# Retention and routed experts on one core: state products as four quarters, and the last chunk's routing logits for all batches together

## The chip, the cores and the metric

The kernel runs on one core of one Trainium2 chip. The metric is the time of the whole program on the device in microseconds (us). Engines: TensorE (PE: products, and PEld: loading of the stationary operand), VectorE (DVE), ScalarE (ACT), GpSimd (POOL) and the SP queue, which issues most DMAs.

## The reference

A retention layer is followed by a mixture of experts. For each of 4 batches and 8 heads a 64 x 64 state decays and takes up one outer product for each of 768 tokens; the output of a token is its query times the state:

```python
for t in range(S):                       # S = 768, D = 64
    state = gamma * state + einsum('bhd,bhe->bhde', k[:, :, t], v[:, :, t])
    y[:, :, t] = scale * einsum('bhd,bhde->bhe', q[:, :, t], state)
```

The 8 heads' outputs of a token, side by side, are a row of 512 numbers. These 3072 rows go to 8 experts:

```python
logits = x @ w_gate                      # 3072 x 8
# all (token, expert) pairs in falling order of logit: a token goes to the first
# expert that still has room (384 rows each)
out[mask] = maximum(x[mask] @ w1[e], 0) @ w2[e]     # 512 -> 1024 -> 512
```

## The kernel before

**Units.** The sequence is cut into 6 chunks `c` of 128 tokens. A unit `u = 4 c + b` is chunk `c` of batch `b`, 24 in all. Heads go in pairs `pr` (4 of them); of a pair, head `s = 0` lies on partitions 0 to 63 and head `s = 1` on 64 to 127. Units 0 to 7 are worked one by one, those after it in pairs (8, 9), (10, 11), ... (22, 23): these are the 16 `groups`. Even places of a pair are even batches, odd ones odd batches.

**One unit** (all in fp32; TensorE works a product in two records in the trace):
- `load` (L256) brings 1 MB of keys, queries and values (768 KB for the last chunk) into one of 8 buffers `ld`, by the SP queue. The load of unit `u + 8` is issued when group work on unit `u` is done.
- `scores` (L288): keys times queries within the chunk, 8 products on 64 rows, `s` choosing the row half; VectorE multiplies the result by the decay mask (`am`, two instructions). GpSimd makes scaled keys `ks` and queries `qs`.
- `outputs` (L316): the part of the outputs that comes from the state. `T[b]` holds for each pair of heads a 128 x 128 block with the two 64 x 64 states on its diagonal and zeros elsewhere, so that one full 128 x 128 product serves both heads. It opens the sums in PSUM tile `yp` (two buffers, one bank each).
- `mix` (L329): scores times values, 8 products with 64 columns, `s` choosing the column half, on top of the same sums. `yp` is copied to `YS[b, c]` (feature by token; of the last chunk half by ScalarE, half by VectorE). The new part of the state, `sp`, is 8 more products, and VectorE adds it to the diagonal of `T[b]` (two instructions a unit, L357).

**Routing.** `gate(c)` (L395) multiplies the outputs of a finished chunk of all four batches by the gate weights `wgf`, 16 products that each fill 32 columns; ScalarE copies the result to `gs`, and `logit` transposes it later, so that logits stand by token. The last chunk goes another way: `gate_last(b)` (L361) takes a batch's `YS` as the stationary operand and 8 gate columns as the moving one, which gives logits by token at once, in units 20 and 21 during the last group and 22 and 23 at the end. Then VectorE takes the maximum of each token, compares it with a grid of 64 thresholds (`reach`) and 24 products count the tokens of each expert above each threshold (L494). A search follows that narrows the threshold twice more (`search`), and its result gives the first expert's rows.

**Rows to memory.** All outputs must lie in memory (`xs`) by token before the experts gather them. 14 units are turned by VectorE's 32 x 32 transposes (`row_blocks`, L384; `ROWS` says how many behind which group) and written by four DMAs of 64 KB each. The other 10 are turned by TensorE beside the search (`rows_out`: four transposes, a ScalarE copy, one DMA of 256 KB); `BESIDE` gives how many units and how many filler products stand before each step of the search. The buffers `xr` are six.

**What sets the order.** TensorE, VectorE and ScalarE follow the order of the code. In a group: scores of the next group, outputs of this one, one step of routing, mix, state, then loads and row transposes. The SP queue issues in the order of the code too; its DMAs take eight semaphores in turn, and each waits until the DMA eight places ahead of it has landed. The experts' stage follows a planner that the change doesn't touch.

Of the kernel before, what the change touches and what calls it, by code (L numbers as in the profile page):

```python
# [43 lines left out]
BESIDE = ((4, 0), (1, 0), (4, 0), (1, 0), (0, 6), (0, 10))  # L44
LEFT = sum(k for k, _ in BESIDE)
# [6 lines left out]
def tile_retention_moe(ctx: ExitStack, tc: tile.TileContext, qkv, wg, idm, w1, w2,  # L52
# [15 lines left out]
    wgf = consts.tile([128, HP, 32], F32, name="wgf")  # L68
# [180 lines left out]
    T = [rc.tile([128, HP, 128], F32, name=f"T{b}") for b in range(B)]  # L249
# [65 lines left out]

    def outputs(us):  # L316

        c = units[us[0]][1]
        for u in us:
            yp = yps[u] = rp.tile([128, HP, C], F32, name="yp", bufs=2)  # L320
            if c:
                b, qs = units[u][0], st[u][1]
                for pr in range(HP):
                    nc.tensor.matmul(yp[:, pr, :], T[b][:, pr, :], qs[:, pr, :], start=(pr == 0), stop=False,  # L324
                                     skip_group_check=True)
            else:
                busy(WARM[u + 1], yp[:, 0:2, :].rearrange("p a b -> p (a b)"))

    def mix(us):  # L329

        c = units[us[0]][1]
        for u in us:
            b, am, yp = units[u][0], st[u][0], yps.pop(u)
            v_ = LD[u][:, 2].rearrange("p (h d) -> p h d", h=H)
            for pr in range(HP):
                for s in range(2):
                    nc.tensor.matmul(yp[64 * s:64 * s + 64, pr, :], v_[:, 2 * pr + s, :], am[:, s, pr, :],  # L337
                                     start=(not c and pr == 0), stop=(pr == HP - 1), skip_group_check=True)
# [6 lines left out]
        if c < NC - 1:  # L345
# [7 lines left out]
            for i, u in enumerate(us):  # L353
                b = units[u][0]
                for s in range(2):
                    r = slice(64 * s, 64 * s + 64)
                    nc.vector.tensor_tensor(T[b][r, :, r], T[b][r, :, r], sp[r, i], op=OP.add)  # L357

    lt5 = []

    def gate_last(b):  # L361
        if not b:
            lt5.append(rp.tile([128, 64, E], F32, name="sp"))
        for pr in range(HP):
            nc.tensor.matmul(lt5[0][:, b, :], YS[b, NC - 1][:, pr, :], wgf[:, pr, 0:E], start=(pr == 0),  # L365
                             stop=(pr == HP - 1))
# [10 lines left out]
    def row_out(pr_, i):  # L377
        b, c = units[i]
        xr = xo.tile([128, DM], F32, name="xr")
        nc.scalar.activation(blocks(xr), pr_.rearrange("p (b a r) -> p b a r", a=4, b=HP), AF.Copy)  # L380
# [3 lines left out]
    def row_blocks(i):  # L384
# [6 lines left out]
        for a in range(4):  # L391
            nc.sync.dma_start(xs[t0:t0 + 128, 128 * a:128 * a + 128].rearrange("(t c) f -> c t f", t=4),
                              xr[32 * a:32 * a + 32].rearrange("p (t f) -> p t f", t=4))

    def gate(c):  # L395

        gl = rp.tile([128, 512], F32, name="gl")
        for pr in range(HP):
            for b in range(B):
                nc.tensor.matmul(gl[32 * b:32 * b + 32, 0:C], wgf[:, pr, :], YS[b, c][:, pr, :], start=(pr == 0),  # L400
# [23 lines left out]
    rowed = 0  # L424
    nu = len(units)
# [23 lines left out]
    with tc.manual_schedule(engines={nc.vector.engine, nc.scalar.engine}):  # L449
# [3 lines left out]
        for g, us in enumerate(groups):  # L453
# [9 lines left out]
            if g > B:  # L463
                if g == len(groups) - 1:
                    for u in groups[g - 1]:
                        gate_last(units[u][0])
# [8 lines left out]
            for _ in range(ROWS.get(g, 0)):  # L475
                row_blocks(rowed)
# [6 lines left out]
        for u in groups[-1]:  # L483
            gate_last(units[u][0])
        c = NC - 1
        cols, Lc = slice(c, COLS, NC), lt5[0][:, 0:B]
        f = best(Lc, cols, m0, oh0)
        reach(cols, B, m0, cmp0, grid[0])
        f()
        c0 = rp.tile([1 << QB[0], E], F32, name="gl")  # L490
        sg0 = sw.tile([1 << QB[0], E], BF, name="sg")
        order = [c for k in range(NC) for c in range(k, COLS, NC)]
        for k, c in enumerate(order):
            nc.tensor.matmul(c0, cmp0[:, c, :], oh0[:, c, :], start=(k == 0), stop=(k == COLS - 1))  # L494
# [409 lines left out]
    def rows_out(i):  # L904
        pr_ = pp.tile([128, DM], F32, name="py" if i % 2 else "ph", bufs=2 if i % 2 else 3)
# [33 lines left out]
    for rows, k in BESIDE:  # L939
        for _ in range(rows):  # L940
            rows_out(rowed)
# [222 lines left out]
```

## Time and profile before

| | us |
|---|---|
| median of 3 runs | 451.43 (449.72 to 455.44) |
| profiled execution | 449.59 |
| its span | 447.7 |
| TensorE busy | 431.4 (96%) |
| VectorE busy | 298.1 (67%) |
| ScalarE, GpSimd busy | 142.9 each (32%) |
| DMA share of q1, the SP queue's / of q0, GpSimd's | 20.5% / 29.9% of 16 engines' span |

The first stage (retention) ends at about 101 us of the span, the search for the first expert runs to 117 us, and the experts fill the rest. In the rows below a time is counted from the start of the span; "L337" is a line of the kernel; an arrow `out<-in` names the tile written and those read. In a timeline row, what stands in brackets at the end is the engine's idle time ahead of the row and what ended it. Matmul rows count records, two for each fp32 product.

### The profile page before, as it was taken

How to read it: one execution, taken by the hardware profiler on the slowest of the kernel's cores; microseconds unless marked ns; L12 is line 12 of the kernel's file. 1: busy time of each engine (PE TensorE's matmuls, PEld its weight loads, DVE VectorE, ACT ScalarE, POOL GpSimd, SP SyncE). 2: the span in 40 equal slices, each digit the busy share in tenths (PEclk: the TensorE clock that was granted, in tenths of full speed). 3: DMA queues.
4: the chain of work that ended last, by engine and by line, in shares of the span. 5: the costliest groups of instructions: out<-in, count | busy, mean ns of one | idle time of the engine just before them, and what ended most of it. 6: DMA issues, size and time to landing. Idle time of an engine off the chain costs nothing.

```text
span 447.7 us, 9118 instructions
## 1 busy us (share of the span) xinstructions
PE 431.4 (96%) x3745; PEld 374.7 (84%) x3747; DVE 298.1 (67%) x714; ACT 142.9 (32%) x221; POOL 142.9 (32%) x154
## 2 busy tenths in 40 slices
PE   8999999899999979999899999999999999999994
PEld 6899999898589758987788799789879989989983
DVE  1668688966989773875876789478678836416500
ACT  1111212115155132423431443343244436326301
POOL 2477655200520360026116016122501615502001
PEclk9999999998999995999999999999999999999998
DMA  7999987745680382038327436513813372831001
GB/s 252 409 416 413 367 272 222 217 90 196 213 281 13 135 280 91 1 119 285 115 94 228 171 119 172 206 49 121 297 77 117 84 294 70 287 160 47 1 25 53
DMA packets 23332, 78.99 MB, mean 176 GB/s; under 512 B 3058, under 2 KB 10866, under 8 KB 16884
## 3 DMA queue, kind: packets, MB, share of 16 engines
q0 software_dynamic: 8592, 46.14, 29.9%
q1 hardware_dynamic: 14692, 32.20, 20.5%
q8 instruction: 31, 0.51, 0.5%
q14 instruction: 17, 0.14, 0.1%
HBM read 65.75 MB, written 12.58 MB: 175 GB/s over the span
## 4 chain that ended last, share of the span: by engine, by line
PE 61%; issue 13%; DMA 12%; DVE 7%; POOL 3%; SPq 1%; ACT 1%; POOLq 0%; DVEq 0%
PE py L888 22%; PE ph L867 22%; DMA ld<-qkv 8%; PE psm L126 5%; PE yp L337 2%; PE pt L835 2%; DMA qtb<-qtab 2%; PE sc L295 2%; DVE w2l L126 2%; PE yp L324 1%; POOL out L896 1%; POOL wraw L783 1%; PE sp L351 1%; DMA xg<-xs,idx 1%; PE sp L365 1%
## 5 line engine op out<-in xcount | busy, mean ns | idle before, releaser
L867 PE MATMUL ph<-xh,w1h 128*128 128x384 f32 x256 | 86.2, 352 | 2.6 <-ACT xh L840 1.8
L867 PE MATMUL ph<-xlo,w1h 128*128 128x384 f32 x256 | 83.9, 341 | 0.0
L867 PE MATMUL ph<-xh,w1l 128*128 128x384 f32 x256 | 83.5, 341 | 0.0
L888 PE MATMUL py<-w2h,hh 128*128 128x512 f32 x192 | 78.4, 408 | 0.0
L888 PE MATMUL py<-w2l,hh 128*128 128x512 f32 x192 | 75.3, 392 | 0.6 <-DVE w2l L126 0.6
L888 PE MATMUL py<-w2h,hl 128*128 128x512 f32 x192 | 75.2, 392 | 0.0
L896 POOL DMA_INDIRECT out<-yo,oix x24 | 27.1, 1131 | 117.7 <-ACT yo L894 116.9
L871 ACT ACTIVATE hh<-ph 128x384 fp32r<-128x384 f32 x64 | 31.4, 491 | 84.4 <-PE ph L867 79.5
L783 POOL DMA_INDIRECT wraw<-w,wix x31 | 36.5, 1179 | 60.4 <-DVE un L126 52.6
L867 PEld LDWEIGHTS ph<-xh,w1h 128*128 128x128 f32 x256 | 48.3, 191 | 4.6 <-ACT xh L840 2.7
L867 PEld LDWEIGHTS ph<-xlo,w1h 128*128 128x128 f32 x256 | 48.6, 192 | 0.0
L867 PEld LDWEIGHTS ph<-xh,w1l 128*128 128x128 f32 x256 | 48.6, 191 | 0.0
L126 DVE SCALAR_TENSOR_TENSOR hl<-ph,hh 128x384 fp32r<-128x384 f32 x64 | 34.8, 552 | 17.1 <-ACT hh L871 16.8
L126 DVE TENSOR_TENSOR w1l<-wraw,w1h 128x1024 fp32r<-128x1024 f32 (+1 forms) x36 | 39.4, 1102 | 7.4 <-ACT w1h L801 7.4
L888 PEld LDWEIGHTS py<-w2l,hh 128*128 128x128 f32 x192 | 36.1, 188 | 7.9 <-DVE w2l L126 1.8
L888 PEld LDWEIGHTS py<-w2h,hl 128*128 128x128 f32 x192 | 36.0, 188 | 7.8
L822 POOL DMA_INDIRECT xg<-xs,idx x24 | 26.5, 1106 | 48.1 <-PE ph L867 34.3
L888 PEld LDWEIGHTS py<-w2h,hh 128*128 128x128 f32 x192 | 36.1, 188 | 6.4
L894 ACT ACTIVATE yo<-py 128x512 f32<-128x512 f32 x24 | 14.3, 598 | 83.9 <-PE py L888 40.2
L126 DVE TENSOR_TENSOR w2l<-wraw,w2h 128x1024 fp32r<-128x1024 f32 x32 | 38.8, 1217 | 1.3 <-ACT w2h L801 1.2
L801 ACT ACTIVATE w1h<-wraw 128x1024 fp32r<-128x1024 f32 (+1 forms) x36 | 33.7, 958 | 11.0 <-DMA wraw<-w,wix 9.4
L801 ACT ACTIVATE w2h<-wraw 128x1024 fp32r<-128x1024 f32 x32 | 33.4, 1053 | 0.0
(149 smaller groups left out, 607.0 us busy)
## 6 DMA issues: line engine op xcount, KB each, us to landing
ld<-qkv SPq DMA_DIRECT2D x19, 1024.0 KB, 10.8
xs<-xr SPq DMA_DIRECT2D x56, 64.0 KB, 3.9
ld<-qkv SPq DMA_DIRECT2D x4, 768.0 KB, 6.2
xs<-xr SPq DMA_DIRECT2D x10, 256.0 KB, 2.9
qtb<-qtab SPq DMA_DIRECT2D x5, 256.0 KB, 12.0
ld<-qkv SPq DMA_DIRECT2D x2, 512.0 KB, 5.5
wraw<-w,wix POOLq DMA_INDIRECT x33, 7.3
xg<-xs,idx POOLq DMA_INDIRECT x24, 3.7
```

Source lines behind the costliest of these rows:

```text
L126: return f(o, *a, **k)
L295: nc.tensor.matmul(sc[s][:, pr, :], k_[r, w], q_[r, w], start=True, stop=True)
L337: nc.tensor.matmul(yp[64 * s:64 * s + 64, pr, :], v_[:, 2 * pr + s, :], am[:, s, pr, :], start=(not c and pr == 0), stop=(pr == HP - 1), s ...
L783: nc.gpsimd.indirect_dma_start(out=t, out_offset=None, in_=w1v if nm == "w1" else w2v, in_offset=bass.IndirectOffsetOnAxis(ap=wix[:, hf:hf ...
L801: nc.scalar.activation(p[0], p[2], AF.Copy)
L822: nc.gpsimd.indirect_dma_start(out=t, out_offset=None, in_=xs, in_offset=bass.IndirectOffsetOnAxis(ap=found[n][0][:, j:j + 1], axis=0))
L835: nc.tensor.transpose(pt[:, d, :], xg[j][:, 128 * d:128 * d + 128], ident)
L867: nc.tensor.matmul(ph, a[:, o:o + 128], x_[:, d], start=(k == 0), stop=(k == 11))
L871: nc.scalar.activation(hh[:, f], ph, AF.Relu)
L888: nc.tensor.matmul(py, h_[:, f, t], a[:, o:o + DM], start=(k == 0), stop=(k == 23))
L894: nc.scalar.activation(yo, py, AF.Copy)
L896: sct = nc.gpsimd.indirect_dma_start(out=out, out_offset=bass.IndirectOffsetOnAxis(ap=oix[:, j:j + 1], axis=0), in_=yo, in_offset=None, bo ...
```

## The change

1. **States without the zeros.** `T[b]` becomes 128 x 4 x 64: head `s` of a pair keeps its 64 x 64 state on its own 64 partitions. A unit's state part of the outputs is 8 products of 64 rows by 64 columns. For even batches head `s` writes partition half `s` of `yp`; for odd batches the other half (`half`), so that the two units of a pair use four different quarters of the array. In a pair the products go by pair of heads, two of the even batch and two of the odd one in turn. The addition to the state is one instruction for a unit.
2. **Odd batches stay exchanged** in `YS`: `mix` writes the exchanged half too; the gate weights get a second copy with its halves exchanged (`wgf` and its load are twice as large); `row_blocks` exchanges the target columns, and `row_out` takes two ScalarE instructions for an odd batch.
3. **Rows.** `TURNED` names the 14 units for VectorE's transposes (odd batches first); the other ten, `rest`, go by TensorE, the first of them (unit 8) already among the last chunk's counts; in `BESIDE` the tenth unit's place holds one filler product.
4. **The last chunk's logits** come from `gate(5)` for all batches, a ScalarE copy and a transpose, as for the other chunks; `gate_last` goes. 20 of the 24 counting products stand around that transpose, four behind it.

The diff, without the host's part and lines that only follow from a name:

```diff
-BESIDE = ((4, 0), (1, 0), (4, 0), (1, 0), (0, 6), (0, 10))
-LEFT = sum(k for k, _ in BESIDE)
+BESIDE = ((4, 0), (1, 0), (4, 0), (0, 1), (0, 6), (0, 10))
+TURNED = (1, 3, 5, 7, 0, 2, 9, 4, 11, 13, 6, 15, 17, 19)
...
-    wgf = consts.tile([128, HP, 32], F32, name="wgf")
+    wgf = consts.tile([128, 2, HP, 32], F32, name="wgf")
...
-    T = [rc.tile([128, HP, 128], F32, name=f"T{b}") for b in range(B)]
+    T = [rc.tile([128, HP, D], F32, name=f"T{b}") for b in range(B)]
...
+    def half(s, b):
+
+        o = 64 * (s ^ (b & 1))
+        return slice(o, o + 64)
+
     def outputs(us):
 
         c = units[us[0]][1]
         for u in us:
-            yp = yps[u] = rp.tile([128, HP, C], F32, name="yp", bufs=2)
-            if c:
+            yps[u] = rp.tile([128, HP, C], F32, name="yp", bufs=2)
+            if not c:
+                busy(WARM[u + 1], yps[u][:, 0:2, :].rearrange("p a b -> p (a b)"))
+        for pr in range(HP if c else 0):
+            for u in us:
                 b, qs = units[u][0], st[u][1]
-                for pr in range(HP):
-                    nc.tensor.matmul(yp[:, pr, :], T[b][:, pr, :], qs[:, pr, :], start=(pr == 0), stop=False,
-                                     skip_group_check=True)
-            else:
-                busy(WARM[u + 1], yp[:, 0:2, :].rearrange("p a b -> p (a b)"))
+                for s in range(2):
+                    r = slice(64 * s, 64 * s + 64)
+                    nc.tensor.matmul(yps[u][half(s, b), pr, :], T[b][r, pr, :], qs[r, pr, :], start=(pr == 0),
+                                     stop=False, skip_group_check=True)
...
-                    nc.tensor.matmul(yp[64 * s:64 * s + 64, pr, :], v_[:, 2 * pr + s, :], am[:, s, pr, :],
+                    nc.tensor.matmul(yp[half(s, b), pr, :], v_[:, 2 * pr + s, :], am[:, s, pr, :],
...
-                for s in range(2):
-                    r = slice(64 * s, 64 * s + 64)
-                    nc.vector.tensor_tensor(T[b][r, :, r], T[b][r, :, r], sp[r, i], op=OP.add)
-
-    lt5 = []
-
-    def gate_last(b):
-        if not b:
-            lt5.append(rp.tile([128, 64, E], F32, name="sp"))
-        for pr in range(HP):
-            nc.tensor.matmul(lt5[0][:, b, :], YS[b, NC - 1][:, pr, :], wgf[:, pr, 0:E], start=(pr == 0),
-                             stop=(pr == HP - 1))
+                nc.vector.tensor_tensor(T[b], T[b], sp[:, i], op=OP.add)
...
-        nc.scalar.activation(blocks(xr), pr_.rearrange("p (b a r) -> p b a r", a=4, b=HP), AF.Copy)
+        to, of = blocks(xr), pr_.rearrange("p (b a r) -> p b a r", a=4, b=HP)
+        if b & 1:
+            for z in range(2):
+                nc.scalar.activation(to[:, :, 2 * z:2 * z + 2], of[:, :, 2 - 2 * z:4 - 2 * z], AF.Copy)
+        else:
+            nc.scalar.activation(to, of, AF.Copy)
...
         for a in range(4):
-            nc.sync.dma_start(xs[t0:t0 + 128, 128 * a:128 * a + 128].rearrange("(t c) f -> c t f", t=4),
+            f0 = 128 * (a ^ 2 * (b & 1))
+            nc.sync.dma_start(xs[t0:t0 + 128, f0:f0 + 128].rearrange("(t c) f -> c t f", t=4),
...
-                nc.tensor.matmul(gl[32 * b:32 * b + 32, 0:C], wgf[:, pr, :], YS[b, c][:, pr, :], start=(pr == 0),
+                nc.tensor.matmul(gl[32 * b:32 * b + 32, 0:C], wgf[:, b & 1, pr, :], YS[b, c][:, pr, :], start=(pr == 0),
...
+    rest = [u for u in range(len(units)) if u not in TURNED]
+    rest.sort(key=lambda u: (u & 1, u))
...
-                if g == len(groups) - 1:
-                    for u in groups[g - 1]:
-                        gate_last(units[u][0])
...
-                row_blocks(rowed)
+                row_blocks(TURNED[rowed])
...
-        for u in groups[-1]:
-            gate_last(units[u][0])
         c = NC - 1
-        cols, Lc = slice(c, COLS, NC), lt5[0][:, 0:B]
+        gate(c)
+        c0 = rp.tile([1 << QB[0], E], F32, name="sc0", bufs=2)
+        order = [c for k in range(NC) for c in range(k, COLS, NC)]
+
+        def first(k0, k1):
+            for k in range(k0, k1):
+                nc.tensor.matmul(c0, cmp0[:, order[k], :], oh0[:, order[k], :], start=(k == 0), stop=(k == COLS - 1))
+
+        first(0, 8)
+        lt = rp.tile([128, 512], F32, name="sp")
+        nc.tensor.transpose(lt[:, 0:128], gs[c % 2], ident)
+        cols, Lc = slice(c, COLS, NC), lt[:, 0:128].rearrange("p (b x) -> p b x", b=B)[:, :, 0:E]
+        first(8, COLS - B)
         f = best(Lc, cols, m0, oh0)
+        pr_ = rp.tile([128, DM], F32, name="sc1", bufs=2)
+        row_part(pr_, rest[0], 0, HP)
+        row_out(pr_, rest.pop(0))
         reach(cols, B, m0, cmp0, grid[0])
         f()
-        c0 = rp.tile([1 << QB[0], E], F32, name="gl")
         sg0 = sw.tile([1 << QB[0], E], BF, name="sg")
-        order = [c for k in range(NC) for c in range(k, COLS, NC)]
-        for k, c in enumerate(order):
-            nc.tensor.matmul(c0, cmp0[:, c, :], oh0[:, c, :], start=(k == 0), stop=(k == COLS - 1))
+        first(COLS - B, COLS)
...
-            rows_out(rowed)
+            rows_out(rest.pop(0), rowed)
```

On TensorE a pair's group around its state products read, before the change (group of units 16 and 17; T_107 and T_108 are the states of batches 0 and 1, `yp` the output sums, L210 a step of routing):

```order
L324 MATMUL yp<-qs,T_107 128x128 x4
L324 MATMUL yp<-qs,T_108 128x128 x4
L210 MATMUL gl<-ident,ext 2x128
L337 MATMUL yp<-am,ld 64x128 x16
L351 MATMUL sp<-ld,ks 64x64 x16
```

and after it, in the same place:

```order
L333 MATMUL yp<-qs,T_107 64x128 x2
L333 MATMUL yp<-qs,T_108 64x128 x2
L333 MATMUL yp<-qs,T_107 64x128 x2
L333 MATMUL yp<-qs,T_108 64x128 x2
L333 MATMUL yp<-qs,T_107 64x128 x2
L333 MATMUL yp<-qs,T_108 64x128 x2
L333 MATMUL yp<-qs,T_107 64x128 x2
L333 MATMUL yp<-qs,T_108 64x128 x2
L210 MATMUL gl<-ident,ext 2x128
L344 MATMUL yp<-am,ld 64x128 x16
L358 MATMUL sp<-ld,ks 64x64 x16
```

Eight whole products of one unit after the other have become 16 products of half width, the two units in turn; what follows stands as before.

At the end of the first stage TensorE had, from the outputs of units 22 and 23 on (ys_5 are the outputs of chunk 5, one tile for each batch):

```order
L324 MATMUL yp<-qs,T_110 128x128 x4
L365 MATMUL sp<-wgf,ys_5_1354 128x8 x4
L365 MATMUL sp<-wgf,ys_5_1365 128x8 x4
L406 MATMUL gl<-ident,gs_142 128x128
L337 MATMUL yp<-am,ld 64x128 x16
L365 MATMUL sp<-wgf,ys_5_1440 128x8 x4
L365 MATMUL sp<-wgf,ys_5_1451 128x8 x4
L494 LDWEIGHTS cmp
L494 MATMUL gl<-oh,cmp 64x8
```

and now (the gate's four rows for the first pair of heads, one for each batch):

```order
L333 MATMUL yp<-qs,T_110 64x128 x2
L408 MATMUL gl<-ident,gs_142 128x128
L344 MATMUL yp<-am,ld 64x128 x16
L402 MATMUL gl<-ys_5_1406,wgf 32x128
L402 MATMUL gl<-ys_5_1417,wgf 32x128
L402 MATMUL gl<-ys_5_1491,wgf 32x128
L402 MATMUL gl<-ys_5_1502,wgf 32x128
```

The 16 products with eight columns, eight of them ahead of the last mix, have become 16 gate products behind it.

On ScalarE the end of the stage read before (ys the copies of the last outputs, xr the first rows beside the search):

```order
L402 ACTIVATE gs_142<-gl 128x128
L341 ACTIVATE ys_5_1440<-yp 128x256
L341 ACTIVATE ys_5_1451<-yp 128x256
L380 ACTIVATE xr<-ph 128x4x4x32
L380 ACTIVATE xr<-py 128x4x4x32
```

and reads now:

```order
L404 ACTIVATE gs_142<-gl 128x128
L348 ACTIVATE ys_5_1491<-yp 128x256
L348 ACTIVATE ys_5_1502<-yp 128x256
L404 ACTIVATE gs_143<-gl 128x128
L381 ACTIVATE xr<-sc_1547 128x4x4x32
L381 ACTIVATE xr<-ph 128x4x4x32
```

A copy of the gate's result has come between the last outputs and the rows, and the first unit of rows stands in a tile of the first stage. VectorE's, GpSimd's and the SP queue's instructions keep their order, but for the merged additions and one exchange on GpSimd (queries of unit 11 ahead of its keys).

## Rows read from the trace of the kernel before

**Rows 1.** Stretches: each engine's busy us, granted TensorE clock, DMA share, GB/s.

```profile
40.00:57.00 17.00, 17.00 (x307) 16.07 (x303) 11.97 (x25) 3.27 (x6) 11.46 (x10) 1.00 0.97 367
68.00:78.00 10.00, 10.00 (x200) 9.32 (x196) 7.99 (x23) 2.42 (x5) 5.47 (x5) 1.00 0.82 237
...
86.30:101.00 14.70, 14.70 (x202) 13.74 (x199) 10.53 (x28) 1.81 (x5) 1.40 (x1) 1.00 0.46 93
102.90:106.30 3.40, 3.40 (x24) 3.07 (x23) 2.43 (x7) 2.19 (x4) 0.00 (x0) 0.50 0.40 148
...
167.80:177.90 10.10, 9.41 (x50) 8.11 (x49) 2.91 (x6) 2.98 (x4) 0.00 (x0) 0.50 0.26 105
```

**Rows 2.** The chain of waits, 28 to 126 us: start, us, what.

```profile
32.28 13.34 DMA ld<-qkv
...
68.32 6.89 DMA ld<-qkv
...
86.41 1.99 PE sc L295 x32
88.39 1.98 PE yp L324 x16
90.37 1.90 PE yp L337 x32
92.27 1.01 PE gl L400 x32
...
95.26 1.69 PE sp L365 x16
...
99.01 1.90 PE sp L365 x16
...
105.87 1.05 PE psm L126 x24
...
108.20 0.44 PE ph L371 x4
...
110.52 0.58 PE py L371 x4
```

**Rows 3.** The SP queue in order of time: start, us, line, DMA, count.

```profile
57.05 0.87 SPq L266 DMA_DIRECT2D ld<-qkv  x2
...
77.80 0.89 SPq L266 DMA_DIRECT2D ld<-qkv  x2
...
86.28 0.30 SPq L392 DMA_DIRECT2D xs<-xr  x1
```

**Rows 4.** The SP queue's waits, 57 to 87 us: total, times, longest.

```profile
SPq L392 <- DMA ld<-qkv: 9.8, 6, 3.2
```

**Rows 5.** GpSimd in order of time: unit 22's queries; the first gather.

```profile
83.46 1.28 POOL L306 TENSOR_TENSOR qs<-ld,qtb 128x512 f32<-128x512 f32 x1 [6.77 <-DMA ld<-qkv]
...
117.03 0.95 POOL L822 DMA_INDIRECT xg<-xs,idx  x1 [0.67 <-DVE idx L126]
```

**Rows 6.** VectorE in order of time, 86 to 111 us.

```profile
86.58 1.71 DVE L357 TENSOR_TENSOR T<-T,sp 64x256 f32<-64x256 f32 x4
88.31 2.48 DVE L298 TENSOR_TENSOR am<-sc,dm 128x512 f32<-128x512 f32 x4
...
100.93 0.19 DVE L126 TENSOR_REDUCE m<-sp 128x4 f32<-128x32 f32 x1 [1.03 <-PE sp L365]
...
102.03 0.16 DVE L126 TENSOR_REDUCE cm<-gl 64x1 f32<-64x8 f32 x1 [0.25 <-PE gl L494]
...
104.14 0.95 DVE L126 TENSOR_TENSOR cmp<-m,th 128x768 bf16<-128x768 f32 x1
...
110.56 0.16 DVE L126 TENSOR_SCALAR sg<-psm 64x8 bf16<-64x8 f32 x1 [0.63 <-PE psm L126]
```

**Rows 7.** TensorE in order of time: its waits at 83 and at 167 us.

```profile
83.20 0.38 PE L216 MATMUL gl<-ident,topb 2*128 2x2 f32 x2 [1.27 <-DVE L L407]
...
167.53 0.88 PE L835 MATMUL pt<-ident,xg 128*128 128x128 f32 x4 [2.53 <-issue]
```

More of the change, by code (lines that the diff above doesn't have):

```diff
@@ L902, in mm2, with rows_out @@
             yield 690
-    def rows_out(i):
-        pr_ = pp.tile([128, DM], F32, name="py" if i % 2 else "ph", bufs=2 if i % 2 else 3)
+    def rows_out(i, k):
+        pr_ = pp.tile([128, DM], F32, name="py" if k % 2 else "ph", bufs=2 if k % 2 else 3)
         row_part(pr_, i, 0, HP)
@@ L1148 @@
     decay, upper, qtab, ktab, thr, cst = _tables()
-    wg = _np.zeros((128, HP, 32), _np.float32)
-    wg[:, :, 0:E] = moe_w_gate.reshape(HP, 128, E).transpose(1, 0, 2)
+    wg = _np.zeros((128, 2, HP, 32), _np.float32)
+    wg[:, 0, :, 0:E] = moe_w_gate.reshape(HP, 128, E).transpose(1, 0, 2)
+    wg[:, 1] = _np.roll(wg[:, 0], 64, axis=0)
     qkv = _np.ascontiguousarray(_np.stack([cols(k), cols(q), rows(v), rows(k)], axis=2))
```

## Prediction

> **What bounds the kernel now.** I read the profile in this order: busy time by stage, the chain of waits of the first stage, then the SP queue and TensorE, and VectorE where the change works.
>
> The change touches the first stage alone, up to 101 us, and the start of the second. In the first stage TensorE is busy without a gap from 40 to 57 and from 68 to 78 us, while the DMA engines are at 0.97 and 0.82 of their time [rows 1]. Two things run side by side, and the question is which would wait if the other were faster. The chain of waits answers it [rows 2]: from 32 to 75 us it lies on loads (13.34 us the first piece, 6.89 the last), and only then goes over VectorE to TensorE.
>
> Why the loads: every DMA of the SP queue waits for the landing of the one eight places ahead. From unit 16 on, two loads are followed by 8 or 12 issues of 64 KB of rows, some of which wait for those two loads, and the next two loads stand behind them. The pair of units 18 and 19 goes out at 57.05 us, that of units 22 and 23, with one pair between, at 77.80 [rows 3]. Between 57 and 87 us SP's row issues waited 9.8 us, six times, for loads [rows 4]. None of it waits for TensorE. The last two loads landed at 83.4 us (unit 22; GpSimd, which waited for it, begins at 83.46, [rows 5]) and 86.3 us (unit 23; the row issue that waited for it goes out at 86.28, [rows 3]). In the chain, TensorE's scores of units 22 and 23 stand from 86.41 [rows 2], 0.1 us behind that landing. So what TensorE gains ahead of 86.3 us is lost in a wait for the load; what it gains behind it counts, down to the first gather for the experts, which waits for VectorE (117.03 us, [rows 5]). The experts' instructions and their order stay, so a gain there is handed through to the end.
>
> **The parts.** *Outputs.* For a pair of units, eight full products become 16 quarter products, 32 records instead of 16. Before, a pair took 1.98 us [rows 2]. What 32 records of quarters take is not in the trace. Near rows, all of 32 records with 128 moving columns [rows 2]: scores, two row halves at a time, 1.99 us; mix, two column halves, 1.90; gate, four column strips, 1.01. So 1.01 if all four quarters run together, 1.9 if two do, and 3.96 (twice 1.98) if none do; no row of this kind is below 1.01, so I take nothing lower. I take 1.01: gate shows four strips at once, scores that row halves overlap, mix that column halves do, and the order puts the four different quarters one behind another. Saved: 0.97 us a pair. A single unit (four of them have a state) has two quarters in 16 records, two at a time as mix's: half of 1.90 against half of 1.98, nothing.
>
> Against this stands a rule of the Trainium skill, TensorEngine Tiling (Array Packing), section Gotcha 1: PSUM Pressure: different row tiles cannot access the same PSUM bank simultaneously. Both quarters of a unit are different row tiles that write one bank, on different partitions; by the rule two quarters of a unit would not run together, and no run here shows it (the scores write a bank for each row half, mix has one row tile). It is rival B below.
>
> *Up to 86.3 us: nothing.* Six pairs save 5.8 us, and TensorE comes to wait for VectorE and for loads instead. Walked through with these rows it is done with units 18 and 19 at about 82.5 us, computes unit 22's scores from 83.4 to 84.4, and waits for unit 23 until 86.3. The larger gate table (64 KB more at the 367 GB/s of [rows 1], 0.2 us) delays the loads behind it by that. VectorE's additions to the state, one for a unit in place of two, and the halved memsets lie beside these waits; they can only shorten.
>
> *From 86.3 us.* Before: scores of both 1.99, outputs 1.98, mix 1.90, gate 1.01, outputs again, the row product of the gate for units 20 and 21 1.69, mix again, that product for units 22 and 23 1.90 [rows 2]; VectorE's maximum at 100.93 [rows 6]. After: scores of unit 23 alone 1.0 (87.3), outputs 1.01 (88.3), mix 1.90 (90.2), gate of chunk 4 1.01 (91.2), outputs 1.01 (92.2), a transpose 0.2 and mix 1.90 (94.3). VectorE's work in this stretch was 10.53 us [rows 1]; the additions (1.71) and unit 22's two of the four masked scores (2.48) [rows 6] now come before it, which leaves 10.53 - 1.71 - 1.24 = 7.6 us, from 87.3 to 94.9, and about 95.2 with two handoffs from ScalarE at the end. So TensorE and VectorE end nearly together. The gate of chunk 5 (1.01) has half its sums ready earlier and ends at 96.1; ScalarE's copy of it 0.3 (an estimate from the like copies of half a tile), the transpose 0.2, handoffs 0.2: the maximum comes at 96.8, **4.1 us earlier**.
>
> *The count.* Before, from the maximum to the read of the counts 1.10 us (100.93 to 102.03, [rows 6]). After, 12 counting products (24 take 1.05) and one unit's transposes (0.58) stand ahead of the last four [rows 2]: 0.53 + 0.58 + 0.18 + 0.1 = 1.4, **0.3 later**.
>
> *The rows beside the search.* Four units' transposes held TensorE until the count of 105.87, though VectorE's comparison for it (104.14, 0.95) was done at 105.1 [rows 2, 6]. The granted clock was 0.50 from 102.9 to 106.3 us, the 1.2 GHz level, behind a stretch of eight-column products [rows 1]; later units took 0.44 to 0.58 [rows 2]. The new order has the gate and a unit's transposes among those products, so I take the full clock: the four are done in time, half of the count's 24 products run ahead of the comparison's second half, **1.2 us earlier** (nothing if the clock falls here too).
>
> *One unit less.* VectorE's threshold was ready at 110.72 [rows 6], but a unit's transposes held TensorE until 111.1 [rows 2]; one filler stands there now: **0.3 earlier**.
>
> *At nothing.* Two ScalarE copies in place of one for units 21 and 23, exchanged column blocks of the same sizes, and the other order of rows: the first gather waits for VectorE and hides them; were it to wait for the rows, 0.3 us.
>
> Sum: -4.1 + 0.3 - 1.2 - 0.3 + 0.2 = -5.1. The profiled execution took 449.6 (its span 447.7): 444.5. The median of the three runs shown, 451.43, lies 1.8 above it; on its scale that is 446.3, and I say **446**.
>
> **The rivals**, on the scale of the median.
>
> A. *The clock falls in the new waits.* At 167.53 us TensorE had idled 2.53 us [rows 7], and the clock stood at 0.50 from 167.8 to 177.9 [rows 1]. The new waits, at about 78, 83 and 85 us, are 0.9 to 2 us each, with work between. Half clock for as long as at 102.9 (3.4 us) costs 1.7, and with the 1.2 of the rows lost the time is 449; as long as at 167.8, it costs 5 and gives 452.5. For it: three waits close together. Against: none is as long as 2.5 us.
>
> The Trainium skill, TensorE: Matmul & The Clock Gate, section HAM oscillation, says that waits for DMAs between bursts of products throttle the clock again. The trace agrees at 167.8 us, behind 2.53 us of idling.
>
> B. *Two quarters at a time; the change doesn't do what it says.* Pairs stay at 1.98; the four single units go from 0.99 to 1.98 if their two quarters exclude each other, 4.0 us, of which a wait that is there now (1.27 us at 83.20, [rows 7]) takes up 1.3. Unit 22's scores begin 2.7 later than now. Behind it two pairs (1.9) and unit 22's scores (1.0) lose their gain: 451.4 + 2.7 - 5.1 + 2.9 = 451.9.
>
> C. *The quarters run one after another* (slower). A pair takes 3.96, 8 x 1.98 more, and the single units 4.0: TensorE is the bound throughout, 19.8 - 1.3, less 2.2 for the rest of the change (5.1 - 2.9): 468. It decides from 2.6 us a pair, where eight pairs lose what the end gains. Against: all near kinds overlap.
>
> D. *The loads come earlier too.* Then the waits for them go, 0.9 and 1.9 us, and with unit 21's about 3.5 in all: 442.8. For: the transposes that feed the row issues come earlier. Against: SP waited for landings, not for them.
>
> **How the numbers follow.** My forecast 0.55 (444 to 448), A 0.24, B 0.08, C 0.04, D 0.09. The predicted time is the likeliest's, 446. The range, 441 to 452, takes in D, B and most of A and leaves out C, the worst of A and the edges, under 2 in 10. 2% is 9 us, about what a measurement of this kernel tells from no change: below 442.4 lie half of D and the low edge of the forecast, 0.09; above 460.5 C, 0.04; between them 0.87.
>
> **What would show it.** Pair outputs of 32 records in 1.0 us; load pairs of the SP queue still at about 57, 68 and 78 us, units 22 and 23 landing at 83 and 86; TensorE idle for some 4.5 us between 77 and 86.5; chunk 5's maximum at 97; transposes beside the search at 0.44 to 0.6 us a unit with the clock at 1.00; the first gather at 112. I am wrong if a pair takes 1.9 us or more, if the last load lands before 85, or if the clock is 0.50 behind 86 us.

## The result, and the profile after

The changed kernel takes 449.85 us (median of 20 runs, 445.64 to 453.43), the kernel before beside it 451.77 (20 runs): a ratio of 0.9926, 95% interval 0.9896 to 0.9955, or 3.3 us less (0.0074 x 451.8). The ratios leave out runs more than 1.5% above the fastest run of their kernel (here four of the changed kernel's 20 and none of the other's); by the medians of all runs the gain is 1.9 us. The forecast was 5.1 us less. The profiled execution took 450.38 us, its span 448.6, longer than that of before; where that comes from is the second half of this section.

The chain of waits of the changed kernel, 60 to 126 us (start, us, what):

```profile
68.61 0.49 DVE xr L389
69.10 7.98 DMA xs<-xr
...
78.46 1.53 SPq L394
80.10 0.37 SPq L266
80.58 6.55 DMA ld<-qkv
87.17 1.16 PE sc L295 x16
88.33 1.03 PE yp L333 x32
89.36 1.90 PE yp L344 x32
91.26 1.01 PE gl L402 x32
...
99.19 0.17 DVE cm L126
...
104.14 0.44 PE ph L367 x4
...
110.86 1.55 PE psm L126 x24
...
113.42 4.24 DMA xg<-xs,idx
...
121.03 1.33 PE ph L878 x3
```

Against [rows 2]: a pair's state part (32 records, L333) takes 1.03 us where it took 1.98. The chain still goes over a load, now by way of a row DMA that stands ahead of it on the SP queue. Chunk 5's counts are read at 99.19 us (102.03 in [rows 6]) and the first gather goes out at 113.42 (117.03 in [rows 5]). The experts' first product stands at 121.03; in the chain of before it was 124.55:

```profile
124.55 0.79 PE ph L867 x3
```

TensorE of the changed kernel in order of time; in brackets the wait ahead of a row:

```profile
80.92 0.38 PE L216 MATMUL gl<-ident,topb 2*128 2x2 f32 x2 [2.85 <-DVE L L409]
81.23 2.55 PE L344 MATMUL yp<-am,ld 128*64 128x128 f32 x32
83.56 1.92 PE L358 MATMUL sp<-ld,ks 128*64 128x64 f32 x32
...
87.17 1.16 PE L295 MATMUL sc<-ld 64*128 64x128 f32 x16 [0.39 <-DMA ld<-qkv]
```

And VectorE:

```profile
77.69 0.71 DVE L389 STREAM_TRANSPOSE xr<-ys 128x512 f32<-128x512 f32 x1 [2.42 <-DMA xs<-xr]
...
97.92 0.19 DVE L126 TENSOR_REDUCE m<-sp 128x4 f32<-128x32 f32 x1 [1.47 <-PE sp L495]
```

TensorE's long wait is not for the load. VectorE waited 2.42 us for one of the six row buffers, whose rows had not landed, and the logits that TensorE needed stood behind that. The load itself cost TensorE 0.39 us.

Stretches of the changed kernel (busy us of PE, PEld, DVE, ACT, POOL; the granted clock; DMA share, GB/s):

```profile
82.50:85.80 3.30, 3.30 (x50) 3.18 (x47) 1.17 (x6) 1.07 (x2) 0.50 (x1) 0.50 0.99 356
102.90:106.30 3.40, 3.40 (x45) 2.97 (x45) 2.54 (x6) 2.67 (x7) 0.00 (x0) 1.00 0.75 269
120.10:126.80 6.70, 6.23 (x21) 5.38 (x20) 5.26 (x12) 3.67 (x8) 2.57 (x3) 0.50 0.76 265
167.90:178.00 10.10, 9.41 (x50) 8.11 (x48) 2.85 (x6) 2.98 (x4) 0.00 (x0) 0.50 0.17 70
```

The clock is 1.00 beside the search, where it was 0.50 [rows 1]. But it is 0.50 at 82.5 us, behind the wait for VectorE, and at 120 us, in the experts' first products. The stretch at 168 us was there before [rows 1]. Of the 3.5 us gained at the experts' first product 2.4 are left at the first copy of a product's result (125.74 against 128.09 us), 1.0 behind the low clock (136.01 against 136.96), and none at 168 us: TensorE waits in both traces for VectorE's `xlo`, which ends at 167.43 and 167.47. Results of TensorE that were read late (last section) go with the 0.9 us by which it ends later.

Twelve runs followed, in sets on different chips; a ratio is to the runs of before in the same set. Their profiles start up to 4 us apart (the clock reaches 1.00 for good at 10 to 13 us in some, at 15 to 17 in those that are late), so they are compared by differences between places of one profile. The runs of before beside them have medians of 449.1 to 451.8 us. "Load to counts" runs from the landing of unit 23's load to the read of chunk 5's counts, "search" from there to the read of the first expert's row numbers (`idx`), "experts" from the experts' first product to the last copy of an output. A dash stands where the loads came well ahead of their use.

| kernel | last load lands | load to counts | search | experts | median us | ratio to before (95%) |
|---|---|---|---|---|---|---|
| before | 86.26 | 15.8 | 14.1 | 317.5 | 451.77 | |
| before, again | 89.62 | 15.6 | 17.2 | 317.6 | 455.96, one run | |
| changed | 87.12 | 12.1 | 13.3 | 321.9 | 449.85 | 0.9926 (0.9896 to 0.9955) |
| changed, again | 87.83 | 12.1 | 12.6 | 313.5 | 446.28 | 0.9929 (0.9892 to 0.9966) |
| quarters alone | 87.14 | 13.9 | 16.5 | 317.8 | 448.95 | 0.9953 (0.9914 to 0.9993) |
| end alone | 87.19 | 14.5 | 12.6 | 317.9 | 447.64 | 0.9954 (0.9906 to 1.0003) |
| one unit after the other | 86.93 | 13.0 | 12.6 | 317.4 | 445.23 | 0.9901 (0.9867 to 0.9936) |
| rows behind the loads | 82.95 | - | 13.2 | 321.2 | 452.29 | 1.0028 (0.9994 to 1.0062) |
| the same in before | 83.27 | - | 16.0 | 317.5 | 453.41 | 1.0034 (1.0002 to 1.0067) |
| eight row buffers | 87.60 | 12.1 | 13.2 | 317.9 | 448.88 | 0.9948 (0.9916 to 0.9980) |
| rows behind, ten buffers | 80.63 | - | 12.6 | 318.7 | 445.19 | 0.9885 (0.9821 to 0.9948) |
| changed, fillers | 89.87 | 12.1 | 12.6 | 313.5 | 442.30 | 0.9845 (0.9789 to 0.9901) |
| before, fillers | 86.23 | 16.2 | 14.1 | 313.2 | 447.12 | 0.9970 (0.9932 to 1.0008) |
| both mends | 80.30 | - | 12.6 | 315.1 | 443.84 | 0.9866 (0.9796 to 0.9936) |

### The profile page after: what moved, and what is told of

Same layout as the page of the kernel before. It is cut to its first block, busy times and chain, and to the rows that moved or that the text cites. A ratio compares the mean times of both kernels' runs of the same rounds, so it can differ in the third digit from the quotient of the medians.

```text
span 448.6 us, 9424 instructions
## 1 busy us (share of the span) xinstructions
PE 427.3 (95%) x3907; PEld 367.5 (82%) x3909; DVE 290.7 (65%) x694; ACT 143.0 (32%) x224; POOL 141.2 (31%) x154
## 4 chain that ended last, share of the span: by engine, by line
PE 67%; issue 13%; DVE 9%; DMA 4%; POOL 2%; ACT 1%; SPq 1%; POOLq 0%; DVEq 0%; ACTq 0%
PE ph L878 22%; PE py L899 21%; PE psm L126 6%; PE sc L295 4%; PE yp L344 3%; PE pt L846 2%; DVE w2l L126 2%; DMA xs<-xr 2%; PE yp L333 2%; DMA ld<-qkv 1%; PE sp L358 1%; POOL out L907 1%; PE gl L312 1%; POOL wraw L794 1%; DVE am L298 1%
## 5 line engine op out<-in xcount | busy, mean ns | idle before, releaser
L878 PE MATMUL ph<-xh,w1h 128*128 128x384 f32 x256 | 87.4, 357 | 2.6 <-ACT xh L851 1.8
L878 PEld LDWEIGHTS ph<-xlo,w1h 128*128 128x128 f32 x256 | 49.5, 195 | 0.1
L298 DVE TENSOR_TENSOR am<-sc,dm 128x512 f32<-128x512 f32 x48 | 29.9, 679 | 7.8 <-PE sc L295 7.8
```

The lines of the kernel that those rows point to most:

```text
L298: nc.vector.tensor_tensor(am[:, s], sc[s], dm[:, s], op=OP.mult)
L878: nc.tensor.matmul(ph, a[:, o:o + 128], x_[:, d], start=(k == 0), stop=(k == 11))
```

## The experiments

**The changed kernel again** (no edit).

> The changed kernel unchanged, beside the others. Theory: the two stretches with a granted clock of 0.50 that its first profile showed at 82.5 and 120 us come from waits that the new kernel always has (VectorE's transposes waiting for a row buffer at 77.7 us, TensorE waiting 1.2 us for the first gathered rows), so they recur within 2 us of these places; the maximum of chunk 5 comes at 97.5 to 98.5 us again. Rival: they belong to the one execution; then at least one of the two is missing here and the span is some 2.5 us shorter for each (448.6 becomes 446 or 443.5). Time: 449.9 by the median of 20 runs, 0.9926 of the kernel before.

Its span was 440.3 us. Two of its stretches:

```profile
81.50:84.80 3.30, 3.30 (x30) 3.29 (x32) 2.09 (x14) 0.60 (x1) 0.00 (x0) 0.50 0.91 248
...
167.90:178.00 10.10, 10.10 (x77) 9.57 (x76) 8.27 (x12) 5.75 (x8) 0.00 (x0) 1.00 0.01 2
```

The low clock at 82 us came again, behind a wait of 2.5 us for VectorE. Those at 120 and 168 us did not, and the experts took 313.5 us in place of 321.9. So the later two belong to the execution: the experts' stage of one program lasts 8.4 us more or less by them. A single profile can't give the time of this change.

**The quarters alone, and the end alone.** The first is the kernel before with parts 1 and 2 of the change: its last logits (with the exchanged copy of the gate weights), `BESIDE` and the order of rows stay. The second is the changed kernel without them, so with parts 3 and 4:

```diff
-    T = [rc.tile([128, HP, D], F32, name=f"T{b}") for b in range(B)]
+    T = [rc.tile([128, HP, 128], F32, name=f"T{b}") for b in range(B)]
...
-        o = 64 * (s ^ (b & 1))
+        o = 64 * s
...
+                nc.tensor.matmul(yps[u][:, pr, :], T[b][:, pr, :], qs[:, pr, :], start=(pr == 0), stop=False,
+                                 skip_group_check=True)
```

> Only the quarters: states without zeros, odd batches exchanged; the last chunk's logits by the old 8-column products, rows in the old order. Theory (the end of the stage was bound by TensorE): two pair outputs behind the last load at 0.97 us saved each, and unit 22's scores (1.0 us) done while unit 23's load is still coming, so that the maximum of chunk 5 comes at 98.0 instead of 100.9 us, and the time is some 2.9 us (0.65 per cent) below before. Rival 1 (VectorE bound, 10.5 us busy behind 86.3 us): the maximum stays at 100.5 to 101 and the time within 0.5 us of before. Rival 2 (what TensorE gains ahead of the last load counts too): the last load lands 3 us earlier and the time falls by 6 us or more.

> Only the end: the last chunk's logits for all batches by the gate's 16 products, counts split, ten rows by TensorE with the first beside the counts; full 128x128 states, no exchange. Theory: from the last load at 86.3 us two row products (1.69 and 1.90 us) give way to one gate of 1.01, with a copy, a transpose and handoffs of 0.7 us: the maximum at 99.2 (1.7 earlier), the rows beside the search at the full clock 1.2 and one row less 0.3, counts 0.3 later: 2.9 us (0.65 per cent) below before. Rival: without the quarters VectorE's additions (1.71 us) and masked scores lie behind the load again and end last; then the maximum stays at 100.5 or later and the time is 0 to 1.5 us below before.

From the last load to the counts the quarters save 1.8 us (15.8 to 13.9) and the end 1.3 (to 14.5); both together save 3.7. The two parts nearly add, and neither rival holds: no load came earlier, and at the maximum VectorE waited for TensorE in both (1.02 and 1.47 us). For the quarters the maximum came at 99.9 us, not 98.0. The load landed 0.9 us later, and behind a wait of 2.72 us for VectorE the clock was 0.50 from 80.2 to 87.0 us:

```profile
81.61 3.68 PE L344 MATMUL yp<-am,ld 128*64 128x128 f32 x32
...
86.92 2.06 PE L295 MATMUL sc<-ld 64*128 64x128 f32 x32
```

So unit 22's scores, 1.0 us, were not done ahead of the load but stand behind it, with unit 23's. The search tells the two parts apart. With the old end its clock is low, here with the quarters:

```profile
100.70:110.80 10.10, 9.65 (x65) 8.90 (x66) 5.61 (x16) 4.56 (x11) 0.00 (x0) 0.50 0.43 154
```

All five profiles with the old end have such a stretch between 100 and 115 us (3.4 to 10.2 us long; the search takes 14.1 to 17.2 us); none of the nine with the new end has one (12.6 to 13.3). The end of the stage, not the quarters, keeps the clock up.

**One unit after the other:** the loops over pairs of heads and over units exchanged.

```diff
-        for pr in range(HP if c else 0):
-            for u in us:
+        for u in us if c else ():
+            for pr in range(HP):
```

> The changed kernel with the state products of a pair written one unit after the other (8 products of the even batch, then 8 of the odd one) instead of in turn. Theory: four quarters run side by side only if four different quarters stand one behind another, so 32 records take 1.9 to 2.0 us instead of 1.03; ahead of the last load that is covered, behind it two pairs cost 1.9 us together, so 1.9 us (0.4 per cent) above the changed kernel, and the last load lands where it did (87 us). Rival 1: TensorE looks far enough ahead and 32 records stay at 1.0 us: no difference. Rival 2: the pairs ahead of the load count as well: eight pairs, 7.7 us above the changed kernel.

TensorE in order of time:

```profile
86.98 1.16 PE L295 MATMUL sc<-ld 64*128 64x128 f32 x16 [1.24 <-DMA ld<-qkv]
88.07 1.59 PE L333 MATMUL yp<-qs,T 64*64 64x128 f32 x32
```

A pair takes 1.59 us where the timeline of the changed kernel shows 1.10 (its chain 1.03): taking turns is worth half a microsecond, but not the whole of what four quarters give. Ahead of the load the six longer pairs cost nothing: the load landed at 86.93. Behind it they cost 0.9 us (13.0 against 12.1). The time is no longer than the changed kernel's (0.9901 against 0.9929, intervals that overlap), so the 1.9 us expected are not there. In this trace TensorE waited 0.35 us for VectorE at 81 us and the clock stayed at 1.00 there; over the 12 runs the mean granted clock is 0.987, over those of the changed kernel beside them 0.984.

**Rows behind the loads**, in the changed kernel and in that before:

```diff
-ROWS = {8: 2, 9: 2, 10: 3, 11: 1, 12: 3, 14: 3}
+ROWS = {8: 2, 9: 2, 11: 4, 12: 3, 14: 3}
```

> The changed kernel with the 12 row DMAs (three units) that stand between the last two pairs of loads moved behind the last pair: ROWS has 4 behind the group of units 14 and 15 in place of 3 and 1. Theory (with the quarters TensorE is bound by the last loads, and these by the row DMAs ahead of them): the last two loads go out 8 to 10 us earlier and land at 77 to 80 us instead of 85 to 88; TensorE does not wait for them; the maximum of chunk 5 comes 3 to 5 us earlier, at 94 to 96 us, and the time is 3 to 5 us (0.7 to 1.1 per cent) below the changed kernel. Rival 1 (something else stands right behind the loads, VectorE with its row transposes and the routing of chunk 4): the loads land earlier but the maximum moves by less than 1 us. Rival 2: the rows, now later, delay the first gather: the time rises.

> The same move of 12 row DMAs in the kernel before. Theory (before the change TensorE had work up to the last load, but for 1.3 us of waiting): the loads land 7 to 9 us earlier here too, but the maximum of chunk 5 moves by 1.3 us at most, from 100.9 to 99.6 or later, and the time falls by 0 to 1.3 us (0 to 0.3 per cent). Rival (both kernels were bound by the loads): the maximum moves as far as in the changed kernel, 3 to 5 us.

The loads landed some 7 us earlier than they would have (this set starts 3 us late), as expected, and the stage became longer. TensorE of the first:

```profile
86.98 0.58 PE L216 MATMUL gl<-ident,topb 2*128 2x2 f32 x2 [6.08 <-DVE L L409]
```

Rows that now stand behind the loads don't land, the six row buffers stay full, VectorE waits for one and TensorE for VectorE. VectorE's wait for a buffer is 4.7 us long. The mechanism is that of rival 1, VectorE with its row transposes, at more than its price. Since the buffers spoil it, the pair says nothing on whether before was bound by the loads.

**Eight row buffers.**

```diff
-    xo = yctx.enter_context(tc.tile_pool(name="xo", bufs=6, side="right"))
+    xo = yctx.enter_context(tc.tile_pool(name="xo", bufs=8, side="right"))
```

> The changed kernel with eight row buffers in place of six. Theory: VectorE's wait of 2.2 to 2.4 us for a row buffer at 77.7 us goes, so TensorE's wait for VectorE at 78.5 us shrinks from 2.5 us and more to under 1 us and the stretch with the clock at 0.50 at 82 us does not come; since the last load still lands at 87 to 88 us the maximum and the time stay within 0.5 us of the changed kernel. Rival: that wait sets the end of the stage; then the maximum comes 1.5 to 2.5 us earlier and the time falls by as much.

TensorE of this kernel:

```profile
82.33 0.38 PE L216 MATMUL gl<-ident,topb 2*128 2x2 f32 x2 [0.84 <-DVE L L409]
...
85.71 1.16 PE L295 MATMUL sc<-ld 64*128 64x128 f32 x16 [0.17 <-DMA ld<-qkv]
```

As expected: VectorE no longer waits for a buffer, TensorE waits 0.84 us for it instead of 2.85, the clock stays up, and load to counts is 12.1 us as before. The time is not better (0.9948). With the wait and the low clock at 82 us and without them the counts follow the load by the same 12.1 us: both are hidden by the load. When the load lands is another matter. This profile starts as late as that of the changed kernel with fillers (below), where the last load lands at 89.87 us; here it lands at 87.60. It was expected to keep its place, and came some 2 us earlier; whether the buffers or the execution did that is open, and the times don't show it.

**The kernel before, again** (no edit).

> The kernel before, unchanged, with a second profile. Theory: the last load lands at 86 to 87 us and the maximum of chunk 5 stands at 100.5 to 101.5 again, so that the later landing in the changed kernel (87.1 and 87.8) belongs to the change; from the first product of the experts to the last output it takes 317.5 us as in the first profile when one low-clock stretch of 10 us falls into it and 313.5 when none does. Rival: the landing varies by a microsecond from execution to execution and comes at 87 or later here too.

The landing, 89.62, is late by the 3 us that this whole profile starts late (its last pair of loads goes out at 81.03, in [rows 3] at 77.80); the counts follow 15.6 us behind it, as in the first profile. Less those 3.2 us the load lands at 86.4, and the kernel before with fillers, which starts in time, has 86.23. The five profiles that start in time and have the larger gate table, with one half of the change or both, have 86.93 to 87.83: in these profiles the later landing goes with the change, and it takes only one half of it. Counted from the landing of unit 21's load it doesn't show: 10.9 to 12.1 us in these five, 11.0 to 11.7 in the three of before.

**Rows behind the loads with ten buffers** (`ROWS` as above, `bufs=10` of the pool `xo`).

> The move of 12 row DMAs behind the last loads, now with ten row buffers in place of six, so that VectorE need not wait for a buffer whose rows stand behind the loads (with six it did: TensorE then waited 6.1 us for the logits of chunk 4). Theory: the last load lands some 6 to 8 us earlier than in the changed kernel (about 79 to 82), TensorE waits neither for it nor for 2 us and more for VectorE between 75 and 90 us, the maximum of chunk 5 comes 2 to 4 us earlier, and the time falls by as much against the changed kernel (ratio to before 0.984 to 0.989). Rival: TensorE's own work is the bound as soon as the loads are early, and the maximum moves by less than 1 us: ratio 0.990 to 0.995.

TensorE at the two places:

```profile
58.75 2.78 PE L295 MATMUL sc<-ld 64*128 64x128 f32 x30 [1.54 <-DVE xr L389]
...
84.95 0.38 PE L216 MATMUL gl<-ident,topb 2*128 2x2 f32 x2 [0.82 <-DVE L L409]
...
88.08 2.06 PE L295 MATMUL sc<-ld 64*128 64x128 f32 x32
```

The last load lands at 80.63 us and TensorE uses it at 88.08 without a wait: the loads bind no more, its own work does. The counts are read at 101.00 us, 0.9 earlier than in the kernel with fillers, which starts as late; but a wait of 1.5 us and a low clock at 60 us lie ahead here. That the counts gain less than 1 us is what the rival said. The ratio, 0.9885, is at the upper end of the theory's range, and its interval takes in the rival's too.

**Fillers in the experts' stage**, in the changed kernel and in that before. `HOT` counts the filler products ahead of the first gathered rows; the 11 new ones stand in the wait at 165 us:

```diff
-HOT = 22
+HOT = 27
...
+        if n == 1 and j == KT - 1 and later is not None:
+            hot = pp.tile([128, 512], F32, name="ph", bufs=3)
+            for _ in range(11):
+                nc.tensor.matmul(hot, onesb, zer512, start=True, stop=True, skip_group_check=True)
```

> The changed kernel with filler products in two waits of the experts' stage: 27 in place of 22 ahead of the first gathered rows, and 11 ahead of the second expert's last turned rows, where TensorE waits 2.5 to 3.0 us for VectorE in every profile so far. Theory: those waits, not the change, give the stretches with the clock at 0.50 at 120 to 132 and at 164 to 184 us; with the fillers neither comes, the time from the experts' first product to the last output is 313 to 314 us (it was 313.5 in the one profile without such a stretch, 317.4 to 317.9 with one, 321.2 and 321.9 with two), and the time falls by 4 us or more against the changed kernel (ratio to before 0.984 or less). Rival: the stretches come all the same, and the ratio stays at 0.993.

> The kernel before with the same fillers in the same two places. Theory: it gains the same 4 us in the experts' stage and keeps the low clock beside the search (102 to 115 us in the profiles of before), so the kernel with the change and the fillers is 5 us (1.1 per cent) below this one, which is the gain worked out for the change alone; ratio to before 0.991. Rival: the low clock in the experts' stage was the same share of the difference between the kernels; then this one falls by more than 6 us and lies within 2 us of the changed kernel with fillers.

Stretches of the changed kernel with fillers:

```profile
164.00:184.00 20.00, 19.08 (x142) 16.49 (x141) 15.32 (x32) 9.11 (x14) 1.39 (x1) 1.00 0.25 95
120.10:126.80 6.70, 6.18 (x58) 5.42 (x57) 5.28 (x12) 3.30 (x7) 3.19 (x4) 1.00 0.70 211
```

The experts take 313.5 and 313.2 us with the clock at 1.00, as expected, and the changed kernel gains 3.8 us by ratio (0.9845 against 0.9929; 4 or more were expected). The mean granted clock says the same of all runs: 0.992 and 0.993 with fillers, 0.985 in the runs of before beside them. This is the fastest kernel measured: 442.30 us, and its interval lies below 1 by more than 0.9%. The kernel before gains less than expected, 0.3% by the ratio where 0.9% was said; by the medians of all runs it gains 2.7 us, 0.6%. Its trace shows the shorter experts' stage; why its times show only a part of it is open. Between the two kernels with fillers the change is worth 4.8 us by the medians (447.12 less 442.30) and 1.25% by the ratios (0.9845 / 0.9970), some 5.6 us.

**Both mends together:** `ROWS` and ten buffers as above, and the fillers.

> The changed kernel with both mends: the 12 row DMAs behind the last loads with ten row buffers, and the fillers in the two waits of the experts' stage. Theory: both gains add, since one lies ahead of 100 us and the other behind 117: the loads land at 80 to 82 us, the counts of chunk 5 are read 1 to 3 us earlier than with the fillers alone (101.94 us there, with a start that was as late), the experts' stage takes 313 to 314 us from its first product to the last output, ratio to before 0.975 to 0.982. Rival: TensorE's own work bounds the first stage as soon as the loads are early, and the ratio is that of the fillers alone, 0.983 to 0.987.

The counts are read at 94.90 us, 5.0 earlier than in the second profile of the changed kernel (99.90), and the row numbers at 107.48. GpSimd's first gather:

```profile
113.42 0.95 POOL L833 DMA_INDIRECT xg<-xs,idx  x1 [5.69 <-DVE cmp L126]
```

What the DMAs of the rows to memory show:

```profile
L383 SPq DMA_DIRECT2D xs<-xr x10: 392/536/600, 101.3 to 106.6; - x10
...
DMA to landing us min/median/max: 1.8/3.1/6.2
```

VectorE had long done the `cmp` that the row names. The last row DMA went out at 106.6 us and landed 6 us later, beside GpSimd's weight gathers of 105.2 and 106.7 us, and the gather needs all rows. It went out at 113.42, where it also stood in both profiles of the changed kernel (113.42 and 113.40). The whole gain of the loads became a wait for the rows. TensorE waited with it, and the fillers were not enough for that wait:

```profile
PE pt L850 <- DMA xg<-xs,idx: 3.4, 1, 3.4
```

Behind it the clock was 0.50 from 117.1 to 127.3 us, and the experts took 315.1 us in place of 313.5. The ratio, 0.9866, is not below that of the fillers alone: the number of the rival, but not for its reason.

## Why the prediction was right, and where its sizes were not

- **Pair outputs: right.** 1.03 us for 1.01 in six of the eight pairs of the first profile, 1.12 and 1.20 in the others. The Trainium skill, TensorEngine Tiling (Array Packing), section Gotcha 1: PSUM Pressure, has different row tiles excluded from one PSUM bank at a time. The trace does not agree: both quarters of a unit write one bank. A pair's 16 records to a bank, taken singly at the 0.12 us of a record before, would last some 1.98 us (an estimate); all 32 took 1.03. A single unit's 16 records, all to one bank, took 1.02. Rivals B and C are out.
- **Nothing gained up to the last load: right, for half its reason.** The longer pairs of the order experiment were free. But TensorE's wait was for VectorE (2.85 us) and the load (0.39) where the walk had 0.9 and 1.9 for loads; the step that failed is that VectorE's work "can only shorten". Its row transposes come earlier and then wait for one of six buffers. The last pair of loads went out at 80.10, not 77.80, and landed 0.86 us later. The term for the gate table said 0.2; with it, five profiles have 0.7 to 1.6. What adds the rest is open: it is there with either half of the change alone.
- **From the load to the counts: right.** -4.1 and +0.3 make -3.8; measured -3.7 against the first profile of before (-3.5 and -4.1 against the two others with this order of loads), in each of the four profiles of this end with the quarters in turn and the loads in their old place (12.1 against 15.8).
- **Rows beside the search, one row less: right.** -1.5 forecast; 14.1 to 12.6 us in the second profile. In the first only 0.8 came of it: 0.7 were lost where a result was read late (below). Against other executions of before, with longer low-clock stretches, it is worth up to 4.6.
- **Handed through to the end: failed, in the first profile wholly.** It held that the experts' stage keeps its length. That stage is 313 to 322 us long by the low-clock stretches of an execution. Rival A's mechanism came at 82 us as described, but its price there is nothing in the changed kernel, since the load hides it; in the quarters alone it cost the 1.0 us of unit 22's scores. The clock that cost the changed kernel time lay at 120 us, which no rival named.
- **The sum.** 5.1 us forecast, 3.3 measured (1.9 by the medians of all runs), 4.8 to 5.6 between the kernels with fillers. The stretch at the experts' start is in three of seven profiles that have the new end and 22 fillers (120, 121 and 126 us) and in none of the four of the old end with 22. It adds some 4 us in two of them (321.2 and 321.9 against 317.5) and 1.2 in the third (318.7), 1.3 us a run over the seven, of the 1.8 that are missing by the ratio. That the change makes the stretch more likely is argued from eleven profiles, not shown. The mean granted clock of all runs does not show it either: 0.980 and 0.984 in the two sets of the changed kernel, 0.982 in the runs of before beside the second.
- **The number.** 446 was said, on the scale of a median of 451.4, and 449.85 measured, inside 441 to 452 but in the band given to rival A, though not for A's reason; the second set of runs gave 446.28 beside 450.3 for before. Within 2%, as the largest chance had it.

The Trainium skill, TensorE: Matmul & The Clock Gate, section HAM oscillation, has waits for DMAs between bursts of products throttle the clock. The kernel with both mends agrees, 0.50 behind a wait of 3.45 us for gathered rows. But most waits here are for VectorE, that of [rows 7] at 167 us too, and a wait's length alone does not tell what follows. In the first stage the clock was 0.50 in or behind waits of 2.51, 2.72, 2.85 and 6.08 us (at 80 to 92 us) and behind one of 1.54 (at 60), and 1.00 behind 0.35 to 1.27 and behind one of 2.35 (rows behind the loads, in before). At 165 us ten of eleven waits of 2.5 to 3.3 us were followed by 0.50, and one of 2.54, in the second profile of the changed kernel, by 1.00. Ahead of the stretch at 120 us stood waits of 0.67, 0.89 and 1.18 us; where it did not come, up to 1.22.

## What to carry to other kernels

Ahead of choosing which products to shorten, find the last wait of the stage and sum only what lies behind it: here the 5.8 us forecast for the products saved ahead of it were worth nothing, and the 3.7 behind the last load counted. When a bound is lifted, look for the next floor on the same data before counting the gain: loads that came 7 us earlier ended in a wait for row buffers, and, with more buffers and fillers, in a wait for the rows themselves. And where the clock falls in some executions only, time the change with that taken out in both kernels; a single profile told the wrong sign.

## What the runs showed of the hardware that was not expected

Four 64 x 64 quarters run side by side although two of them write one PSUM bank, and how far depends on the order of the products: by the timelines 1.10 us a pair in turn, 1.59 unit by unit, 2.05 as full products.

A result of TensorE was sometimes read late. In the first profile of the changed kernel VectorE read the counts that give `idx` at 112.50 us, 0.83 us behind the last product's recorded end, where it was 0.11 in the trace of before; later, at 205 and 209 us, VectorE and ScalarE were 1.4 us late. Five of the fourteen profiles have this, of both kernels, and the others none. Four of the five are all the profiles of one set on one chip, and the eight profiles of the three other sets have none, so it may go with the chip; what causes it is open.
